# Lo weights 112 bytes into their tiles for K and Q, and a new order of the products of K, G and Q, in a two-layer linear-attention and MLP kernel

## The chip, the cores and the metric

One core of one Trainium2 chip runs the whole program. Times are device microseconds of one execution. Before the change three runs took 870.21, 870.62 and 871.27 us, median 870.62.

## The reference, cut to what matters

An input of 2048 tokens of 448 features passes twice through an attention block and an MLP block, each behind a layer norm and with a residual. The attention is linear: no softmax, a sum over all tokens of phi(k) times v, 16 heads of 28.

```
def A(x, wqkv, wo):                      # S = 2048, D = 448, H = 16, Dh = 28
    q, k, v = split(x @ wqkv)
    phi = lambda t: where(t > 0, t + 1, exp(t)) + 1e-6
    pq, pk = phi(q), phi(k)
    kv = einsum("bhsd,bhse->bhde", pk, v)
    z = einsum("bhsd->bhd", pk)
    o = einsum("bhqd,bhde->bhqe", pq, kv) / (einsum("bhqd,bhd->bhq", pq, z) + 1e-6)
    return o @ wo

def B(x, w1, b1, w2, b2):                # F = 1792
    return gelu(x @ w1 + b1) @ w2 + b2

for _ in range(2):
    x = x + A(layernorm(x), wqkv, wo)
    x = x + B(layernorm(x), w1, b1, w2, b2)
```

All is float32.

## The kernel before

**Products in pieces.** TensorE multiplies fp32r operands here. To keep the accuracy of float32, each operand is split into hi (rounded) and lo (the rest), and a product is made as hi*hi + hi*lo + lo*hi in one accumulator in PSUM. The 448 rows of a contraction are taken as three chunks of 128 and a tail of 64; in the tail the 128 rows hold hi and lo of one side, stacked, so that it needs two products and not three. A product of one tile is thus 3 x 3 + 2 = 11 matmuls.

**Which side is the weights.** Each matmul loads 128x128 weights and streams the other operand past them. For K and Q the weights are turned (transposed) tokens and the matrix streams, 448 columns; for G, which is tokens transposed times phi(k), the weights are the tokens as they are; in the MLP's second half (y) and in the output product of attention (op) they are turned activations. In the MLP's first half (hp) the matrix is the weights and 512 tokens stream.

**Phase 1.** For each layer and each of 16 tiles of 128 tokens, `phase1` (from L610) makes the layer norm, turns the tile, and issues K(t) (`stage_k`, through `proj`, L321), the transposes of tile t+1 if that tile is turned on TensorE (only tiles 0 to 7 of layer 0, `TURNED`), G(t-1) (`stage_g`, L522) and Q(t) (`stage_q`). The order within a step is written out in `STEP` and `STEPS`, one token for one stage. Q is made in the loop for tiles 0 to 8 only; the Q's of the last seven tiles fill gaps of the transition (`ORDER`, tokens Q and Qa), where K and V are combined with the output matrix.

**Other tiles are turned by VectorE and DMA.** `turn` transposes 32x32 blocks (L299, L300), `store_sq` writes two tiles to DRAM (L305) and `spread` reads them back so that the blocks are in place (L311). `split_t` (L313) then makes hi on ScalarE (XH, L317) and lo on VectorE (XL, L318). For tiles turned on TensorE this is `split_x` (L272, L273).

**Where the pieces lie.** XH and XL (class `Block`, L228) hold four tiles each, two buffers; the same tags serve the turned tokens of the MLP (key "m"), where XL streams. Tiles of tags B and F are 576 elements wide and can be used from element `APART` = 28 on, that is 112 bytes in: so lie xnl (lo of the tokens for G, L446), ql and gl. XL starts at its tile's start.

**Order of products before.** `proj` goes through the chunks: hi by the matrix's hi, hi by its lo, lo by its hi, so that lo weights come third, sixth, ninth and eleventh of eleven. G does the same for three chunks, and its last chunk has two products with hi weights, since there hi and lo of the tail share one tile: lo comes third, sixth and ninth. For the tile before the last two (`t == NT - 3`, L526) G has an order of its own, which stays.

Of the kernel before, what the change touches and what calls it, by code (L numbers as in the profile page):

```python
# [9 lines left out]
F32 = mybir.dt.float32  # L10
F32R = mybir.dt.float32r
# [11 lines left out]
def linear_attn_mlp_kernel(  # L23
# [12 lines left out]
    pe, act, dve, pool, sp = nc.tensor, nc.scalar, nc.vector, nc.gpsimd, nc.sync  # L36
# [4 lines left out]
    H, DH = 16, 28  # L41
    NT = S // 128
# [4 lines left out]
    TL = D - 64  # L47
    LAYERS = 2

    consts = ctx.enter_context(tc.tile_pool(name="consts", bufs=1))  # L50
    wts = ctx.enter_context(tc.tile_pool(name="wts", bufs=1))
    work = ctx.enter_context(tc.tile_pool(name="work", bufs=2))
# [9 lines left out]
    def bank(tag, bufs, name):  # L62
        return psum.tile([128, 512], F32, name=name, tag=tag, bufs=bufs)
# [7 lines left out]
    APART = 28  # L71
# [24 lines left out]
    wkq = {}  # L96
# [90 lines left out]
                       compare_op=OP.is_ge, fill=0.0)  # L187
    b1s = consts.tile([128, NF], F32, name="b1s")
    b2b = consts.tile([128, D], F32, name="b2b")
    consts.tile([128, 48], F32, name="space")  # L190

    w1h = wts.tile([128, 3, F], F32R, name="w1h")
    w1l = wts.tile([128, 3, F], F32R, name="w1l")
# [9 lines left out]


    def ln_bn(xs):
        st = work.tile([128, 6], F32, name="bst", tag="bst", bufs=3)
        dve.bn_stats(st, xs)
        return st

    def ln_stats(xs, st=None):  # L210
        st = ln_bn(xs) if st is None else st
        mv = work.tile([128, 2], F32, name="bmv", tag="bmv", bufs=3)
        dve.bn_aggr(mv, st)
        ve = work.tile([128, 1], F32, name="bve", tag="bve", bufs=3)
        dve.tensor_scalar(ve, mv[:, 1:2], 1e-5, None, op0=OP.add)  # L215
        rs = work.tile([128, 1], F32, name="brs", tag="brs", bufs=3)
        pool.tensor_tensor(rs, ve, mhalf, op=OP.pow)  # L217
        return xs, mv, rs

# [6 lines left out]


    class Block:  # L228
        def __init__(self):
            self.hi = work.tile([128, 2048], F32R, name="XH", tag="XH", bufs=2)  # L230
            self.lo = work.tile([128, 2048], F32R, name="XL", tag="XL", bufs=2)

        def pieces(self, t):

# [11 lines left out]
    blocks = {}  # L246

    def block(key):
        if key not in blocks:
            blocks[key] = Block()  # L250
        return blocks[key]

    tps = {}
# [1 line left out]
    def transpose_x(xn, tail, key, j, tag="m"):  # L255

        block(key)
        tp = tps[key, j] = bank(tag, 4 if tag == "acc" else 2, "tp")
        for c in range(4):
            pe.transpose(tp[:, c * 128:(c + 1) * 128], xn[:, c * 128:(c + 1) * 128] if c < 3 else tail, ident)  # L260

    def transpose_halves(xn, tail, key, j):

        block(key)
        tps[key, j] = [bank("acc", 4, "tp") for _ in range(2)]
        for c in range(4):
            pe.transpose(tps[key, j][c // 2][:, c % 2 * 128:][:, :128], xn[:, c * 128:(c + 1) * 128] if c < 3 else tail, ident)
# [26 lines left out]
    def turn(x, key, t):  # L294
        x = x[:, :D]
        if (key, t // 2) not in squares:
            squares[key, t // 2] = half("sq")
        sq = squares[key, t // 2].rearrange("p (m c u n) -> p c m u n", m=4, c=4, n=32)[:, :, :, t % 2]
        dve.transpose(sq[:, :3], x[:, :TL].rearrange("p (c m n) -> p c m n", c=3, n=32))  # L299
        dve.transpose(sq[:, 3].rearrange("p (u m) n -> p u m n", u=2),  # L300
                      x[:, TL:].rearrange("p (m n) -> p m n", n=32)[:, None].to_broadcast([128, 2, 2, 32]))

    def store_sq(key, h):
        d = stored[key, h] = dram([128, 1024], F32, f"sq_{'_'.join(map(str, key))}_{h}")
        sp.dma_start(d, squares.pop((key, h)))  # L305

    def spread(key, h):
        r = spreads[key, h] = half("sp")
        d = stored.pop((key, h)).rearrange("(i r) (m f) -> m r i f", i=4, m=4)
        for m in range(4):  # L310
            sp.dma_start(r[m * 32:(m + 1) * 32].rearrange("r (i f) -> r i f", i=4), d[m])  # L311
# [6 lines left out]
        eng.tensor_tensor(lo.rearrange("p (c i n) -> p c i n", c=4, n=32), x, f(h), op=OP.subtract)  # L318


    def proj(name, key, j, o=None, cs=range(4)):  # L321
        if o is None:
            o = bank("m" if name == "k" else "h", 2, "ps" + name)[:, :D]
        b = blocks[key]
        for c in cs:
            if c < 3:
                hi, lo = wkq[name, c]
                pe.matmul(o, b.still(b.hi, j, c), hi, start=(c == 0), stop=False)  # L328
                pe.matmul(o, b.still(b.hi, j, c), lo, start=False, stop=False)  # L329
                pe.matmul(o, b.still(b.lo, j, c), hi, start=False, stop=False)  # L330
            else:
                pe.matmul(o, b.still(b.hi, j, 3), wkq[name, 3], start=False, stop=False)
                pe.matmul(o, b.still(b.lo, j, 3), wkq[name, 3], start=False, stop=True)
        return o
# [71 lines left out]
    def stage_a(l, t):  # L406
        sts[l, t] = ln_stats(xt.pop((l, t)))
# [16 lines left out]
    def stage_sp(l, t):  # L424
        if t >= TURNED[l]:
            block(("a", l, t // 4))
            spread(("a", l, t // 4), t % 4 // 2)
# [23 lines left out]

    ko = {}

    def stage_k(l, t, cs=range(4)):
        ko[l, t] = proj("k", ("a", l, t // 4), t % 4, ko.get((l, t)), cs)

    def stage_kphi(l, t):
        o = ko.pop((l, t))
# [36 lines left out]
    qs_ = {}  # L495

    def stage_q(l, t, cs=range(4), tag=None):
        if tag:
            qs_[l, t] = bank(tag, 4, "psq")[:, :D]
        qs_[l, t] = proj("q", ("a", l, t // 4), t % 4, qs_.get((l, t)), cs)  # L500
        if 3 in cs:
            qo.append((l, t, qs_.pop((l, t))))

# [18 lines left out]
    def stage_g(l, t, acc):  # L522
        h, lo = split.pop((l, t))
        kh, kl = ks.pop((l, t))
        first, last = t == 0, t == NT - 1
        if t == NT - 3:  # L526

            for c in range(4):
                pe.matmul(acc[c], h[:, c * 128:(c + 1) * 128], kh, start=False, stop=False)
            for c in range(3):  # L530
                pe.matmul(acc[c], lo[:, c * 128:(c + 1) * 128], kh, start=False, stop=False)
            for c in range(4):
                pe.matmul(acc[c], h[:, c * 128:(c + 1) * 128], kl, start=False, stop=False)
            return
        for c in range(3):
            s = slice(c * 128, (c + 1) * 128)
            pe.matmul(acc[c], h[:, s], kh, start=first, stop=False)  # L537
            pe.matmul(acc[c], h[:, s], kl, start=False, stop=False)  # L538
            pe.matmul(acc[c], lo[:, s], kh, start=False, stop=last)
        pe.matmul(acc[3], h[:, TL:], kh, start=first, stop=False)  # L540
        pe.matmul(acc[3], h[:, TL:], kl, start=False, stop=last)

# [211 lines left out]
    def q_scale(l, b, j, tr):  # L756
        pq = pqt[l, b * 4 + j]
        pz = pzs.pop((l, b, j))
        dn = work.tile([128, H], F32, name="dn", tag="dn", bufs=2)
        dve.tensor_reduce(dn, pz.rearrange("p (h d) -> p h d", d=DH), axis=mybir.AxisListType.X, op=OP.add)  # L760
        dve.tensor_tensor(dn, dn, tr.dc, op=OP.add)
        rd = work.tile([128, H], F32, name="rd", tag="rd", bufs=2)
        dve.reciprocal(rd, dn)
        p3 = pq.rearrange("p (h d) -> p h d", d=DH)
        dve.scalar_tensor_tensor(p3, p3, 1e-6, rd[:, :, None].to_broadcast([128, H, DH]),
                                 op0=OP.add, op1=OP.mult)
# [62 lines left out]
    def m_split(l, b, j):  # L829

        if j < 2:
            split_t(("m", l, b), j, *block(("m", l, b)).pieces(j), dve if j else pool)
        else:
            split_x(("m", l, b), j)
# [150 lines left out]

    table(AF.Exp)
    stage_a(0, 0)
    work.tile([128, 32], F32, name="space", tag="space", bufs=1)
    bn = ln_bn(xt[0, 1])
    split_hi("k", 0, st_k)  # L990
    stage_n(0, 0)
# [4 lines left out]
    for l in range(LAYERS):  # L996
        tr = SimpleNamespace(mp={})
        za, acc = phase1(l, tr)
# [9 lines left out]
        def pre(j):  # L1008
# [4 lines left out]

        tok_ = SimpleNamespace(
            Q=lambda j: stage_q(l, fill.pop(0)), Qp=lambda j: fill_qphi(), Qv=lambda j: stage_qphi(j or 9),
            Qa=lambda j: stage_q(l, fill.pop(0), tag="acc"), G=lambda j: stage_g(l, NT - 1, acc),
            ld=lambda j: (load_pq(l, 0, j), load_x(l, j)), z=lambda j: trans_z(tr, zs[l]), gt=lambda j: trans_gt(tr, acc),
# [4 lines left out]
            x=lambda j: m_split(l, 0, j), tu=lambda j: turn(xns.pop(("m", l, j)), ("m", l, 0), j),  # L1022
            st=lambda j: store_sq(("m", l, 0), 0), sp=lambda j: spread(("m", l, 0), 0), pre=pre, b=biases)
        for tok in ORDER.split():
            name, j = tok.rstrip("0123456789"), int("0" + tok.lstrip("abcdefghijklmnopqrstuvwxyzQTG"))
# [6 lines left out]
        for b in range(NB):  # L1032
            acc = [bank("acc", 4, f"y{j}")[:, :D] for j in range(4)]
# [5 lines left out]
            for i in range(NF):  # L1039
# [12 lines left out]
                elif l + 1 < LAYERS:  # L1052
# [4 lines left out]
                    if i in (3, 4, 6, 7, 8):  # L1057
                        t = (3, 4, 6, 7, 8).index(i)
# [36 lines left out]
```

## Time and profile before

| | |
|---|---|
| runs | 870.21, 870.62, 871.27 us |
| profiled execution | 870.69 us, of which the span of instructions 869.0 us |
| TensorE busy | 863.5 us, 4182 matmuls (each float32 one that is not a transpose counts twice) |
| VectorE, ScalarE, GpSimd busy | 491.6, 344.7, 221.5 us |
| K, G and Q of layer 0 | from 7 to about 137 us |
| K, G and Q of layer 1 | from 438 to about 564 us |

In the rows of groups stand line, engine, operation, out<-in by the program's names, shapes and count, then busy us, mean ns of one, and the idle time of the engine ahead of them. Rows of the timeline begin with the start in us from the span's start and the duration. PE is a matmul, PEld the load of its weights, SPq a DMA issued by SyncE. Matmuls are pipelined: a record of 360 ns doesn't mean that the next starts 360 ns later.

### The profile page before, as it was taken

To read this page: it belongs to the slowest core of one execution; us is meant where nothing else is said; L and a number is where in the kernel's file an instruction comes from. 1 tells how busy PE (TensorE), PEld (TensorE's weight loads), DVE (VectorE), ACT (ScalarE), POOL (GpSimd) and SP (SyncE) were. 2 spreads that over 40 slices of the span, in tenths; PEclk is the share of its full clock that TensorE was granted. 3 is DMA by queue.
4 is the path that set the end of the run, shared out by engine and by line. 5 is a ranking of instruction groups with operands and counts; after the bars stand their busy time and mean duration, and the time that the engine had idled before them with its cause. 6 is when DMAs were issued, how large, how long until landed. Compare 5 with 4: busy or idle time off the path is not lost.

```text
span 869.0 us, 11679 instructions
## 1 busy us (share of the span) xinstructions
PE 863.5 (99%) x4182; PEld 771.0 (89%) x4182; DVE 491.6 (57%) x958; ACT 344.7 (40%) x606; POOL 221.5 (25%) x250
## 2 busy tenths in 40 slices
PE   9999999999999999999999999999999999999998
PEld 8999888888888888888899998888888888888887
DVE  6888496658456443226477876864674483533112
ACT  6776635324323322333355665342233133223231
POOL 5566532235012102012222344120220140140000
PEclk9999999999999999999999999999999999999999
DMA  5474736624313402051145443252332413111001
GB/s 160 139 234 158 210 89 205 193 89 131 134 60 105 158 0 98 1 181 49 49 145 184 165 133 106 98 182 90 105 115 92 129 68 125 49 49 42 1 1 43
DMA packets 63642, 94.76 MB, mean 109 GB/s; under 512 B 8928, under 2 KB 58720, under 8 KB 63584
## 3 DMA queue, kind: packets, MB, share of 16 engines
q1 hardware_dynamic: 63408, 93.87, 33.6%
q8 instruction: 33, 0.54, 0.3%
q14 instruction: 25, 0.20, 0.1%
q10 hardware_dynamic: 176, 0.14, 0.0%
HBM read 56.17 MB, written 34.60 MB: 104 GB/s over the span
## 4 chain that ended last, share of the span: by engine, by line
PE 98%; DMA 0%; DVE 0%; ACT 0%; POOL 0%; issue 0%; SPq 0%; DVEq 0%; ACTq 0%
PE y L895 10%; PE y L894 10%; PE y L896 10%; PE hp L863 9%; PE hp L861 9%; PE hp L862 9%; PE hp L865 3%; PE hp L864 3%; PE psk L329 2%; PE psq L329 2%; PE psq L328 2%; PE psq L330 2%; PE psk L330 2%; PE psk L328 2%; PE G L538 2%; PE G L537 2%
## 5 line engine op out<-in xcount | busy, mean ns | idle before, releaser
L871 DVE TENSOR_TENSOR gl<-g,gh 128x512 fp32r<-128x512 f32 x112 | 83.2, 743 | 294.4 <-ACT gh L870 294.4
L867 ACT ACTIVATE g<-hp,b1s 128x512 f32<-128x512 f32 x112 | 77.1, 688 | 400.9 <-PE hp L865 392.6
L895 PE MATMUL y<-w2l,gh 128*128 128x448 f32 x447 | 163.6, 366 | 0.0
L894 PE MATMUL y<-w2h,gh 128*128 128x448 f32 x447 | 162.0, 362 | 0.0
L896 PE MATMUL y<-w2h,gl 128*128 128x448 f32 x447 | 160.0, 358 | 0.0
L863 PE MATMUL hp<-XL,w1h 128*128 128x512 f32 x336 | 130.9, 390 | 0.0
L862 PE MATMUL hp<-XH,w1l 128*128 128x512 f32 x336 | 130.7, 389 | 0.0
L861 PE MATMUL hp<-XH,w1h 128*128 128x512 f32 x336 | 130.7, 389 | 0.0
L217 POOL TENSOR_TENSOR brs<-bve,mhalf 128x1 f32<-128x1 f32 x64 | 39.4, 616 | 281.0 <-DVE bve L215 277.9
L894 PEld LDWEIGHTS y<-w2h,gh 128*128 128x128 f32 x447 | 83.7, 187 | 9.4
L895 PEld LDWEIGHTS y<-w2l,gh 128*128 128x128 f32 x447 | 83.9, 188 | 7.0
L896 PEld LDWEIGHTS y<-w2h,gl 128*128 128x128 f32 x447 | 84.0, 188 | 5.0
L863 PEld LDWEIGHTS hp<-XL,w1h 128*128 128x128 f32 x336 | 63.1, 188 | 13.6 <-issue 0.6
L861 PEld LDWEIGHTS hp<-XH,w1h 128*128 128x128 f32 x336 | 63.0, 187 | 10.6
L862 PEld LDWEIGHTS hp<-XH,w1l 128*128 128x128 f32 x336 | 63.1, 188 | 9.9
L870 ACT CAST gh<-g 128x512 fp32r<-128x512 f32 x112 | 69.6, 622 | 3.6
L754 POOL TENSOR_TENSOR pz<-pq,zb 128x448 f32<-128x448 f32 x32 | 36.7, 1148 | 81.9 <-DVE dn L760 61.0
L448 POOL TENSOR_TENSOR xnl<-x,xnh 128x384 fp32r<-128x384 f32 x32 | 35.2, 1099 | 72.1 <-ACT xnh L447 40.1
L318 DVE TENSOR_TENSOR XL<-sp,XH 128x512 fp32r<-128x512 f32 x50 | 44.6, 898 | 4.3 <-ACT XH L317 4.3
L865 PE MATMUL hp<-XL,w1x 128*128 128x512 f32 x112 | 43.6, 389 | 0.0
L864 PE MATMUL hp<-XH,w1x 128*128 128x512 f32 x112 | 43.6, 389 | 0.0
L823 POOL TENSOR_TENSOR x<-x,b2b 128x448 f32<-128x448 f32 x32 | 41.9, 1331 | 0.0
(169 smaller groups left out, 1565.2 us busy)
## 6 DMA issues: line engine op xcount, KB each, us to landing
x<-in_A_x_dram SPq DMA_DIRECT2D x32, 224.0 KB, 4.0
pq_d<-eq SPq DMA_DIRECT2D x32, 224.0 KB, 2.7
pq<-pq_d SPq DMA_DIRECT2D x32, 224.0 KB, 3.3
sq_m<-sq SPq DMA_DIRECT2D x14, 512.0 KB, 2.8
sp<-sq_m SPq DMA_DIRECT2D x56, 128.0 KB, 2.8
x<-x_d SPq DMA_DIRECT2D x32, 224.0 KB, 3.4
sq_a<-sq SPq DMA_DIRECT2D x12, 512.0 KB, 2.9
sp<-sq_a SPq DMA_DIRECT2D x48, 128.0 KB, 3.1
```

Of the source, the lines that this page charges most:

```text
L318: eng.tensor_tensor(lo.rearrange("p (c i n) -> p c i n", c=4, n=32), x, f(h), op=OP.subtract)
L861: pe.matmul(o, w1h[:, c, s], x.moving(x.hi, c), start=(c == 0), stop=False)
L862: pe.matmul(o, w1l[:, c, s], x.moving(x.hi, c), start=False, stop=False)
L863: pe.matmul(o, w1h[:, c, s], x.moving(x.lo, c), start=False, stop=False)
L864: pe.matmul(o, w1x[:, s], x.moving(x.hi, 3), start=False, stop=False)
L865: pe.matmul(o, w1x[:, s], x.moving(x.lo, 3), start=False, stop=True)
L867: act.activation(g, hp, AF.Gelu_apprx_tanh, bias=b1s[:, i:i + 1])
L870: act.copy(gh, g)
L871: dve.tensor_sub(gl, g, f(gh))
L894: pe.matmul(acc[j], gh[:, s], w2h[:, i], start=first, stop=False)
L895: pe.matmul(acc[j], gh[:, s], w2l[:, i], start=False, stop=False)
L896: pe.matmul(acc[j], gl[:, s], w2h[:, i], start=False, stop=stop)
```

## The change

XL's tile becomes 64 elements wider, and blocks of attention (key "a") use it from element 28 on, blocks of the MLP from its start. The products of K and Q of a whole tile, and those of G, are put in an order by tables: a list of the hi products and one of the lo products is merged so that lo products come at given places of the eleven. Which places is given by layer and tile (`k_at`, `q_at`, `g_at`). Taken through K, G and Q of a step in which nothing stands between them, these places are every third: in layer 1, tile 3, K has lo at 2, 5, 8, 11, G at 3, 6, 9, Q at 1, 4, 7, 10. K of tiles 10 to 15 starts with lo. The parts of K and Q that are issued chunk by chunk for the first two tiles of layer 0 keep their order.

Room is found elsewhere: the small tiles of the layer norm's statistics and the denominator move to another pool, the denominator has one buffer and not two, and two unused spacers go.

```diff
-    consts.tile([128, 48], F32, name="space")
...
-        st = work.tile([128, 6], F32, name="bst", tag="bst", bufs=3)
+        st = consts.tile([128, 6], F32, name="bst", tag="bst", bufs=3)
...
     class Block:
-        def __init__(self):
+        def __init__(self, at):
             self.hi = work.tile([128, 2048], F32R, name="XH", tag="XH", bufs=2)
-            self.lo = work.tile([128, 2048], F32R, name="XL", tag="XL", bufs=2)
+            self.lo = work.tile([128, 2112], F32R, name="XL", tag="XL", bufs=2)[:, at:at + 2048]
...
-            blocks[key] = Block()
+            blocks[key] = Block(APART if key[0] == "a" else 0)
...
+    def merge(his, los, at):
+
+        his, los = iter(his), iter(los)
+        return [next(los if i + 1 in at else his) for i in range(11)]
+
-    def proj(name, key, j, o=None, cs=range(4)):
+    def proj(name, key, j, o=None, cs=range(4), at=(3, 6, 9, 11)):
         if o is None:
             o = bank("m" if name == "k" else "h", 2, "ps" + name)[:, :D]
         b = blocks[key]
+        if len(cs) == 4:
+            w = [wkq[name, c] for c in range(3)]
+            his = [(b.still(b.hi, j, c), p) for c in range(3) for p in w[c]] + [(b.still(b.hi, j, 3), wkq[name, 3])]
+            los = [(b.still(b.lo, j, c), w[c][0]) for c in range(3)] + [(b.still(b.lo, j, 3), wkq[name, 3])]
+            for i, (x, p) in enumerate(merge(his, los, at)):
+                pe.matmul(o, x, p, start=(i == 0), stop=(i == 10))
+            return o
...
+    def k_at(l, t):
+        if t < 9:
+            return ((2, 5, 8, 11) if t == 2 else (3, 6, 9, 11)) if l == 0 or t == 0 else (2, 5, 8, 11)
+        return (2, 5, 8, 11) if t == 9 else (1, 4, 7, 10)
+
+    def q_at(l, t):
+        if t < 9:
+            return (2, 5, 8, 11) if l == 0 and t < 8 else (2, 4, 7, 10) if t == 0 else (1, 4, 7, 10)
+        return (2, 5, 8, 11) if t == 10 else (3, 6, 9, 11) if t in (12, 13) else (1, 4, 7, 10)
+
+    def g_at(l, t):
+        if t < 9:
+            return (4, 7, 10) if l == 0 and t < 7 else (3, 6, 9)
+        return (4, 7, 10) if t == NT - 1 else (2, 5, 8)
...
-        for c in range(3):
-            s = slice(c * 128, (c + 1) * 128)
-            pe.matmul(acc[c], h[:, s], kh, start=first, stop=False)
-            pe.matmul(acc[c], h[:, s], kl, start=False, stop=False)
-            pe.matmul(acc[c], lo[:, s], kh, start=False, stop=last)
-        pe.matmul(acc[3], h[:, TL:], kh, start=first, stop=False)
-        pe.matmul(acc[3], h[:, TL:], kl, start=False, stop=last)
+        x = [h[:, c * 128:(c + 1) * 128] for c in range(3)] + [h[:, TL:]]
+        his = [(c, x[c], k) for c in range(4) for k in (kh, kl)]
+        los = [(c, lo[:, c * 128:(c + 1) * 128], kh) for c in range(3)]
+        made = merge(his, los, g_at(l, t))
+        for i, (c, w, k) in enumerate(made):
+            others = [m[0] for m in made[:i]], [m[0] for m in made[i + 1:]]
+            pe.matmul(acc[c], w, k, start=first and c not in others[0], stop=last and c not in others[1])
...
-        dn = work.tile([128, H], F32, name="dn", tag="dn", bufs=2)
+        dn = consts.tile([128, H], F32, name="dn", tag="dn", bufs=1)
...
-    work.tile([128, 32], F32, name="space", tag="space", bufs=1)
```

More of the change, by code (lines that the diff above doesn't have):

```diff
@@ L211, in ln_stats @@
         st = ln_bn(xs) if st is None else st
-        mv = work.tile([128, 2], F32, name="bmv", tag="bmv", bufs=3)
+        mv = consts.tile([128, 2], F32, name="bmv", tag="bmv", bufs=3)
         dve.bn_aggr(mv, st)
-        ve = work.tile([128, 1], F32, name="bve", tag="bve", bufs=3)
+        ve = consts.tile([128, 1], F32, name="bve", tag="bve", bufs=3)
         dve.tensor_scalar(ve, mv[:, 1:2], 1e-5, None, op0=OP.add)
-        rs = work.tile([128, 1], F32, name="brs", tag="brs", bufs=3)
+        rs = consts.tile([128, 1], F32, name="brs", tag="brs", bufs=3)
         pool.tensor_tensor(rs, ve, mhalf, op=OP.pow)
@@ L452, in linear_attn_mlp_kernel @@
     ko = {}
+    def k_at(l, t):
[10 more added lines that the diff above has]
+        return (4, 7, 10) if t == NT - 1 else (2, 5, 8)
     def stage_k(l, t, cs=range(4)):
-        ko[l, t] = proj("k", ("a", l, t // 4), t % 4, ko.get((l, t)), cs)
+        ko[l, t] = proj("k", ("a", l, t // 4), t % 4, ko.get((l, t)), cs, k_at(l, t))
     def stage_kphi(l, t):
@@ L499, in stage_q @@
             qs_[l, t] = bank(tag, 4, "psq")[:, :D]
-        qs_[l, t] = proj("q", ("a", l, t // 4), t % 4, qs_.get((l, t)), cs)
+        qs_[l, t] = proj("q", ("a", l, t // 4), t % 4, qs_.get((l, t)), cs, q_at(l, t))
         if 3 in cs:
```

## The prediction

> **What bounds the kernel now.** I read the page first, parts 1, 2 and 4.
>
> ```profile
> span 869.0 us, 11679 instructions
> ...
> PE 863.5 (99%) x4182; PEld 771.0 (89%) x4182; DVE 491.6 (57%) x958; ACT 344.7 (40%) x606; POOL 221.5 (25%) x250
> ...
> PEclk9999999999999999999999999999999999999999
> ...
> PE 98%; DMA 0%; DVE 0%; ACT 0%; POOL 0%; issue 0%; SPq 0%; DVEq 0%; ACTq 0%
> ```
>
> TensorE is busy all the time, at its full clock, and 98% of the chain that ended last is matmuls, so the time is the number of products times the distance from one to the next. The change removes no product. What it can change is that distance, and I looked for a place where products of the same size follow each other at two paces. The groups by line, shapes kept apart:
>
> ```profile
> L328 PE MATMUL psq<-wq,XH 128*128 128x448 f32 x96 | 35.6, 371 | 0.0
> ...
> L329 PE MATMUL psq<-wq,XH 128*128 128x448 f32 x96 | 35.1, 366 | 0.0
> L330 PE MATMUL psq<-wq,XL 128*128 128x448 f32 x96 | 35.0, 365 | 0.0
> L537 PE MATMUL G<-kh,xnh 128*128 128x448 f32 x90 | 33.4, 371 | 0.0
> ...
> L539 PE MATMUL G<-kh,xnl 128*128 128x448 f32 x90 | 32.5, 361 | 0.0
> L804 PE MATMUL op<-wq,qh 128*128 128x448 f32 x72 | 26.4, 366 | 0.0
> L803 PE MATMUL op<-wq,qh 128*128 128x448 f32 x72 | 26.1, 362 | 0.0
> L805 PE MATMUL op<-wq,ql 128*128 128x448 f32 x72 | 25.8, 358 | 0.0
> ...
> L332 PE MATMUL psq<-wq,XH 128*128 128x448 f32 x32 | 11.7, 367 | 0.0
> ```
>
> Q (psq) and the output product (op) move the same wq buffers, 448 columns past 128x128 weights, in the same order hi, hi, lo. By the code they differ in one thing: ql lies 28 elements, 112 bytes, into its tile, XL at its start. op's records last 366, 362 and 358 ns in turn, Q's 371, 366 and 365. G, whose xnl also lies 112 bytes in, stands between. The records overlap, so I take the pace from starts, in the timeline. First y, which also runs hi, hi, lo with an offset lo, then K, where one step of the loop (K, G and Q of 11 products each, 33 together) repeats:
>
> ```profile
> 302.41 0.36 PE L894 MATMUL y<-w2h,gh 128*128 128x448 f32 x1
> ...
> 304.81 0.39 PE L861 MATMUL hp<-XH,w1h 128*128 128x512 f32 x1
> ```
> ```profile
> 462.93 0.36 PE L328 MATMUL psk<-wk,XH 128*128 128x448 f32 x1
> ...
> 496.33 0.36 PE L328 MATMUL psk<-wk,XH 128*128 128x448 f32 x1
> ```
>
> Twelve products of y take 2.40 us, 200 ns each. Five steps, 165 products, take 33.40 us, 202.4 ns each. So there are 2.4 ns a product to be had in K, G and Q. The same order of G is found at two paces:
>
> ```profile
> 51.69 0.36 PE L539 MATMUL G<-kh,xnl 128*128 128x448 f32 x1
> ...
> 52.29 0.36 PE L539 MATMUL G<-kh,xnl 128*128 128x448 f32 x1
> ...
> 52.89 0.36 PE L539 MATMUL G<-kh,xnl 128*128 128x448 f32 x1
> ```
> ```profile
> 76.30 0.36 PE L539 MATMUL G<-kh,xnl 128*128 128x448 f32 x1
> ...
> 76.91 0.36 PE L539 MATMUL G<-kh,xnl 128*128 128x448 f32 x1
> ...
> 77.53 0.36 PE L539 MATMUL G<-kh,xnl 128*128 128x448 f32 x1
> ```
>
> From lo to lo it is 0.60 us here (200 ns a product) and 0.615 there (205 ns), within one G each: an offset lo at every third place gives a cycle that keeps itself, and whether it is the good or the bad one is settled by how the sequence is entered. The change puts the offset into K and Q and lines up the three products so that the cycle need not be entered again each time.
>
> **The change part by part.** K and Q have 3x96 and 2x32 products each over both layers (x96 and x32 above), 352, and G as many, one for each of K's; 1056 in all.
>
> Layer 1's loop, nine full steps and seven of K and G alone: some 430 products. With lo exactly at every third place through K, G and Q I take y's 200.0, that is 2.4 ns less. In the seven later steps 22 products hold 7 lo's, so one distance is four; that breaks the cycle once a step, and I take 2.2 ns over the whole: 430 x 2.2 = 0.95 us.
>
> Layer 0's loop up to the K of tile 9: seven steps have four transposes between K and G. G after them is in the good cycle already (the rows at 51.69), so only K and Q gain, 22 products x 2.4, less what K's last three lose on the way into the transposes: 0.055 us a step, 0.4 in seven. The two steps without transposes gain 33 x 2.4 = 0.08 each, of which I count 0.1 together. Sum 0.5 us.
>
> Layer 0 from there to the K of tile 14 is held by something else:
>
> ```profile
> 91.29 0.19 PEld L328 LDWEIGHTS psk<-wk,XH 128*128 128x128 f32 x1
> ...
> 91.84 0.19 PEld L330 LDWEIGHTS psk<-wk,XL 128*128 128x128 f32 x1
> ...
> 93.97 0.50 PEld L529 LDWEIGHTS G<-kh,xnh 128*128 128x128 f32 x3 [0.41 <-ACT kh L465]
> ```
> ```profile
> 91.50 0.36 PE L328 MATMUL psk<-wk,XH 128*128 128x448 f32 x1
> ...
> 91.91 0.40 PE L330 MATMUL psk<-wk,XL 128*128 128x448 f32 x1
> ```
> ```profile
> 91.09 0.69 DVE L318 TENSOR_TENSOR XL<-sp,XH 128x512 fp32r<-128x512 f32 x1 [2.40 <-ACT XH L317]
> ```
> ```profile
> 90.44 0.62 ACT L317 CAST XH<-sp 128x512 fp32r<-128x512 f32 x1 [2.49 <-DMA sp<-sq_a]
> ```
> ```profile
> 85.72 1.75 SPq L311 DMA_DIRECT2D sp<-sq_a  x4
> ```
>
> XL of tile 14 is finished at 91.78, because its turned tokens come late from the DMA issued at 85.72; the load of the first lo weights waits to 91.84 for it. ACT's queue is held by the same DMA, so its kh for G of tile 13 is late too, and PE waits 0.41 us there. TensorE coming sooner doesn't move these: the 88 products of four steps after the K of tile 9 gain 0.2 us that I count at nothing, the late XL being their cover; without it they are worth 0.2 more. Here the change also puts lo first in K, two products sooner. Its load would be due at about 91.29 and still goes at 91.84, so K's first product starts where its third did, 0.4 us later, with all of K queued behind it on PE, and behind K its Relu and Exp, and G. G is then due 0.4 us later too, which is the 0.41 us that its loads now wait for kh: that wait falls away. A product after a late load comes soon behind it (91.91 after 91.84, where 91.50 after 91.29 shows the usual 0.2), so a wait of 0.4 us costs PE less than 0.4. From both sides: 0 lost if the wait gives all back, 0.4 if nothing; I take 0.1 lost, near the row of the wait.
>
> The other K's of tiles 10 to 15 have lo first too. In layer 1 there is room:
>
> ```profile
> 503.05 0.82 DVE L318 TENSOR_TENSOR XL<-sp,XH 128x512 fp32r<-128x512 f32 x1
> ```
> ```profile
> 505.26 0.36 PE L328 MATMUL psk<-wk,XH 128*128 128x448 f32 x1
> ```
>
> XL is done 1.4 us ahead of K, and two products are 0.4. Tile 15 of layer 0 is near its limit:
>
> ```profile
> 95.02 1.14 DVE L318 TENSOR_TENSOR XL<-sp,XH 128x512 fp32r<-128x512 f32 x1
> ```
> ```profile
> 96.31 0.36 PE L328 MATMUL psk<-wk,XH 128*128 128x448 f32 x1
> ```
>
> XL ends at 96.16, K's first load is due 0.2 ahead of 96.31, at 96.1; K starting 0.1 later by the loss above, the two meet. It costs from 0 to 0.1; I take 0.
>
> After the loops: G of tile 15 and seven Q's in each layer, in layer 0 K of tile 15 and a G more: 110 and 88 products between transposes and other products. At 2.3 ns 0.25 and 0.2 us. The first two tiles of layer 0 keep the old order but get the offset; 30 products there are not behind a wait, 0.06 us.
>
> Nothing is charged for the rest. DVE writes gl 112 bytes in already and takes no longer for it, and it idles 43%; dn with one buffer is written and read by DVE alone, in order; the statistics only move in SBUF.
>
> ```profile
> L871 DVE TENSOR_TENSOR gl<-g,gh 128x512 fp32r<-128x512 f32 x112 | 83.2, 743 | 294.4 <-ACT gh L870 294.4
> ...
> L318 DVE TENSOR_TENSOR XL<-sp,XH 128x512 fp32r<-128x512 f32 x50 | 44.6, 898 | 4.3 <-ACT XH L317 4.3
> ```
>
> Sum: 0.95 + 0.5 - 0.1 + 0.25 + 0.2 + 0.06 = 1.86 us less. The profiled execution took 870.69 us (869.0 of span and 1.7 around it), 0.07 above the median of the three runs, 870.62; so 868.8.
>
> **A rule against it.** op's lo at 358 ns against Q's at 365, on the same moving tiles, says that the place of the weights matters. The Trainium skill, page "SBUF — State Buffer", section "Who interferes with whom", gives TensorE two independent read ports, one for the moving operand and one for weights, and its "Specifications (TRN2)" speak of 16-byte lines, of which 112 bytes are a whole number. By that page the offset could change nothing, and the sum would be that of the third rival below. The rows speak against it, but they compare different stages.
>
> **The rivals.** First, slower: the bad cycle. If the long sequence is entered as G was at 76.30, it stays there, since nothing breaks it any more; 205 in place of 202.4 ns over some 900 products in loops and tails is +2.3 us, 872.9. With a share f in the bad cycle the change is 2.4(1-f) - 2.6f a product, so it turns slower from f = 0.48 on. For it: that stretch. Against: y, op and most of G after transposes are found in the good one.
>
> Second, the good cycle is lost at each boundary, or at each break of three, and found again only after several products, as in G now; half the gain, 0.9 us, 869.7. For it: K's late lo and the transposes break it for certain. Against: in layer 1's nine full steps nothing stands between K, G and Q.
>
> Third, the offset does nothing in K and Q and what differs between Q and op is something else of their stages. Then only order changes, and with the 0.1 us of tile 14 it is 870.7. Against it G, which stands between K and Q in the same stage and has the 361 ns.
>
> **How the numbers follow.** Forecast 0.64, bad cycle 0.08, half 0.22, nothing 0.06. What a measurement can tell from no change is about 0.2%, 1.74 us, so the line is at 868.9, close to the forecast. Its own spread is from 868.0 (2.4 ns on all 1056 products, and 0.1 for the rest) to 869.4; I put four fifths of it under the line: 0.51, the rest of it with the second and third rival and half of the first within: 0.45; slower 0.04. The range 868.0 to 870.3 takes in the second rival and leaves out the first and most of the third.
>
> **What would show it.** Starts of psk rows 6.60 us apart in layer 1's full steps in place of 6.68; mean records of the lo products of K and Q at 358 ns; G's 371 down to 362 to 366. The load of the first lo weights of tile 14 waiting for XL, and the wait for kh after it shorter. The bad cycle would show as lo to lo 0.61 us over whole steps; the third rival as steps that stay at 6.68. A new wait of PE for XL elsewhere, or steps that gain while the span doesn't, would prove me wrong on what covers what.

## The result, and the profile after

| | before | after |
|---|---|---|
| runs, median | 871.07 us (869.93 to 872.39, 22 runs) | 869.54 us (868.91 to 870.74, 22 runs) |
| profiled execution | 870.69 us | 869.28 us |
| its span | 869.0 us | 867.5 us |

The ratio of the times is 0.9985, with a 95% interval of 0.9978 to 0.9991: about 1.3 us less. Parts 1 and 4 of the page of after:

```profile
span 867.5 us, 11673 instructions
...
PE 862.3 (99%) x4182; PEld 771.1 (89%) x4182; DVE 492.0 (57%) x958; ACT 345.0 (40%) x606; POOL 221.9 (26%) x250
...
PE 96%; DVE 1%; DMA 1%; ACT 1%; issue 0%; POOL 0%; SPq 0%; DVEq 0%; ACTq 0%; POOLq 0%
```

The same 4182 products keep TensorE busy for 1.2 us less. The chain that ended last has 1% each of DMA, ScalarE and VectorE in it, which were at 0%: on its way back it now leaves TensorE at one place, which is K of tile 14 in layer 0, below. K and Q have one line now, so the groups part by hi and lo (columns as before: busy us, mean ns of one, idle ahead):

```profile
L334 PE MATMUL psq<-wq,XL 128*128 128x448 f32 x120 | 43.7, 364 | 0.0
...
L334 PE MATMUL psk<-wk,XL 128*128 128x448 f32 x120 | 43.3, 361 | 0.3 <-DVE XL L317 0.3
...
L567 PE MATMUL G<-kh,xnl 128*128 128x448 f32 x90 | 32.3, 359 | 0.0
```

These means mix good stretches and bad ones. The pace is in the starts. The first products of the same two K's of layer 1, five steps apart, in the timeline of after:

```profile
462.17 0.37 PE L334 MATMUL psk<-wk,XH 128*128 128x448 f32 x1
...
495.17 0.37 PE L334 MATMUL psk<-wk,XH 128*128 128x448 f32 x1
```

33.00 us where it was 33.40: 6.60 a step, 200.0 ns a product. And a K from within, lo after lo:

```profile
462.97 0.36 PE L334 MATMUL psk<-wk,XL 128*128 128x448 f32 x1
...
463.57 0.36 PE L334 MATMUL psk<-wk,XL 128*128 128x448 f32 x1
...
464.17 0.36 PE L334 MATMUL psk<-wk,XL 128*128 128x448 f32 x1
```

0.60 us from lo to lo throughout, the good cycle of the prediction: behind a lo the next products start after 196, 199 and 205 ns. By stage, from the starts of K in both traces (K2 is the first product of K of tile 2, hp the first product of the MLP):

| stretch | before, us | after, us | difference |
|---|---|---|---|
| start of span to K2, layer 0 | 20.07 | 19.93 | -0.14 |
| K2 to K9, layer 0 | 49.13 | 48.80 | -0.33 |
| K9 to K15, layer 0 | 27.10 | 27.07 | -0.03 |
| K15 to hp, layer 0 | 41.31 | 41.31 | 0.00 |
| hp to K0 of layer 1 | 300.78 | 300.83 | +0.05 |
| K0 to K15, layer 1 | 84.69 | 83.73 | -0.96 |
| K15 to hp, layer 1 | 41.32 | 41.25 | -0.07 |
| hp of layer 1 to end of span | 304.57 | 304.62 | +0.05 |

Two thirds of the gain come from layer 1's loop. The two stretches of the MLP, which the change leaves as they were, take 300.74 to 300.85 and 304.54 to 304.65 us over the kernels here (three executions apart, named below), so 0.05 us there says nothing. Two stretches show the bad cycle in place of the good one. One begins with the G behind a dummy transpose in the step of tile 7 and lasts through G(6), Q(7) and K(8), 57.5 to 64.3 us; three lo's of K(8), in the timeline of after:

```profile
62.48 0.36 PE L334 MATMUL psk<-wk,XL 128*128 128x448 f32 x1
...
63.10 0.36 PE L334 MATMUL psk<-wk,XL 128*128 128x448 f32 x1
...
63.71 0.36 PE L334 MATMUL psk<-wk,XL 128*128 128x448 f32 x1
```

0.61 to 0.62 us from lo to lo (about 203, 203 and 208 ns), 204.6 ns a product over Q(7) and over K(8), each of which had some 202.6 before. The other is the Q's of tiles 12 and 13 in both layers, behind op. The first product of a Q and the first of op after it, in the timeline of after and then of before:

```profile
124.88 0.57 PE L334 MATMUL psq<-wq,XH 128*128 128x448 f32 x2
...
127.14 0.37 PE L818 MATMUL op<-Mh,qh 112*128 112x448 f32 x1
```
```profile
125.39 0.37 PE L328 MATMUL psq<-wq,XH 128*128 128x448 f32 x1
...
127.62 0.36 PE L792 MATMUL op<-Mh,qh 112*128 112x448 f32 x1
```

The eleven products take 2.25 us where they took 2.23, and the twelve of op behind them 202.8 ns each, where it was 200.2. So the tails give back there what other Q's gain.

Tile 14 of layer 0, the rows of ScalarE, VectorE, the weight loads and TensorE in the timeline of after:

```profile
89.84 0.62 ACT L316 CAST XH<-sp 128x512 fp32r<-128x512 f32 x1 [2.43 <-DMA sp<-sq_a]
```
```profile
90.49 0.69 DVE L317 TENSOR_TENSOR XL<-sp,XH 128x512 fp32r<-128x512 f32 x1 [2.35 <-ACT XH L316]
```
```profile
91.23 0.19 PEld L334 LDWEIGHTS psk<-wk,XL 128*128 128x128 f32 x1 [0.67 <-DVE XL L317]
...
93.36 0.80 PEld L555 LDWEIGHTS G<-kh,xnh 128*128 128x128 f32 x4
```
```profile
91.24 0.47 PE L334 MATMUL psk<-wk,XL 128*128 128x448 f32 x1 [0.29 <-DVE XL L317]
```

The first load of K, now lo, waits 0.67 us for XL, which ends at 91.18 because XH waited for the DMA; G's loads after it wait for kh no more (0.41 us before).

### The profile page after: what moved, and what is told of

Same layout as the page of the kernel before. It is cut to its first block, busy times and chain, and to the rows that moved or that the text cites. A ratio compares the mean times of both kernels' runs of the same rounds, so it can differ in the third digit from the quotient of the medians.

```text
span 867.5 us, 11673 instructions
## 1 busy us (share of the span) xinstructions
PE 862.3 (99%) x4182; PEld 771.1 (89%) x4182; DVE 492.0 (57%) x958; ACT 345.0 (40%) x606; POOL 221.9 (26%) x250
## 4 chain that ended last, share of the span: by engine, by line
PE 96%; DVE 1%; DMA 1%; ACT 1%; issue 0%; POOL 0%; SPq 0%; DVEq 0%; ACTq 0%; POOLq 0%
PE y L921 10%; PE y L920 10%; PE y L922 10%; PE hp L889 9%; PE hp L887 9%; PE hp L888 9%; PE psq L334 8%; PE psk L334 6%; PE G L567 6%; PE hp L890 3%; PE hp L891 3%; PE op L830 2%; PE op L829 2%; PE op L831 2%; PE op L819 1%; PE op L818 1%
## 5 line engine op out<-in xcount | busy, mean ns | idle before, releaser
L334 PE MATMUL psq<-wq,XH 128*128 128x448 f32 x210 | 62.2, 365 | 0.0
L334 PE MATMUL psk<-wk,XH 128*128 128x448 f32 x210 | 61.9, 364 | 0.0
L567 PE MATMUL G<-kh,xnh 128*128 128x448 f32 x120 | 44.5, 371 | 0.0
```

The lines of the kernel that those rows point to most:

```text
L334: pe.matmul(o, x, p, start=(i == 0), stop=(i == 10))
L567: pe.matmul(acc[c], w, k, start=first and c not in others[0], stop=last and c not in others[1])
```

## The experiments

All traces below were read in the same way: first products of K of layer 1's tiles 4 and 9 (five steps, 165 products), and the table's stretches. Three executions (at16, bad_entry, dummies3) are some 0.5 us longer in each of two stretches, with no cause in their edits: K15 to hp of layer 0 (41.75 to 41.82 us, where the same stretch of layer 1 takes 41.24 to 41.31) and hp to K0 of layer 1 (301.35 to 301.39 us). So single times are not compared, the loops are.

### The two parts alone: offset_only and order_only

The first keeps XL 112 bytes in and goes back to the old places of lo; the second keeps the new order and puts XL at its start.

```diff
     def k_at(l, t):
+        return (3, 6, 9, 11)
...
     def q_at(l, t):
+        return (3, 6, 9, 11)
...
     def g_at(l, t):
+        return (3, 6, 9)
```

> XL 112 bytes in for K and Q, but K, G and Q in the order of before (lo third, sixth, ninth, and eleventh in K and Q). Theory (offset and unbroken every-third together): K and Q now have lo, one hi, lo at their end, which breaks the cycle twice a step, so it is left and found again; a full step of layer 1 (33 products) takes 6.62 to 6.66 us, between 6.60 of the changed kernel and 6.68 of before, and about half of the gain is left: some 0.8 us less than before. Rival that the offset alone does it: steps of 6.60 and at least the whole gain, 1.5 us, since K of tile 14 also doesn't wait longer. Rival that the order alone does it: 6.68, no gain.

```diff
-            blocks[key] = Block(APART if key[0] == "a" else 0)
+            blocks[key] = Block(0)
```

> The new order of K, G and Q with XL at its tile's start again. Theory: only G has offset lo weights, 3 of 33, so nothing keeps the cycle over K and Q: a full step of layer 1 stays within 6.66 to 6.70 us, K and Q at 202 to 203 ns a product, and the time is that of before or up to 0.3 us over it, because the wait of K of tile 14 for XL stays two products earlier. Rival that the order alone does it: 6.60 us a step and 1.5 us less than before.

offset_only: 870.83 us over 11 runs, ratio 0.9994 (0.9985 to 1.0003). order_only: 870.75 us over 11 runs, ratio 0.9997 (0.9988 to 1.0006). Neither can be told from no change by time alone; the traces part them. The first products of the two K's, offset_only and then order_only:

```profile
462.79 0.57 PE L334 MATMUL psk<-wk,XH 128*128 128x448 f32 x2
...
496.09 0.57 PE L334 MATMUL psk<-wk,XH 128*128 128x448 f32 x2
```
```profile
462.49 0.36 PE L334 MATMUL psk<-wk,XH 128*128 128x448 f32 x1
...
495.89 0.36 PE L334 MATMUL psk<-wk,XH 128*128 128x448 f32 x1
```

The offset alone gives 33.30 us, a quarter of the 0.40 that the change brings here (over the whole loop of layer 1 84.39 us against 84.69, a third); the order alone 33.40, which is nothing, and with it the tiles that were moved to make room are worth nothing here, since order_only has them moved too. So the third rival falls: the place of the weights matters. And the old places of lo, where the distance from lo to lo is two at the end of K and Q and five from G to Q, lose most of it, more than the half that was expected. The gain needs both parts.

### Is it the 112 bytes? at32, at16, at24

The order of the change, with XL 128, 64 and 96 bytes in.

```diff
-            blocks[key] = Block(APART if key[0] == "a" else 0)
+            blocks[key] = Block(32 if key[0] == "a" else 0)
```

at16 and at24 have 16 and 24 in that place.

> The changed kernel with XL 32 elements, 128 bytes, in and not 112. Theory (what counts is where in a line of 128 bytes or less the lo weights begin, against hi): as XL at 0, steps of 6.66 to 6.70 us. Rival (any place other than the tile's start, or a place away from XH, is enough): 6.60 us.

> The changed kernel with XL 16 elements, 64 bytes, in. If a line of 64 bytes or less is what counts, as XL at 0: 6.66 to 6.70 us a step; if one of 128 bytes, another value, 6.60 if every shift helps.

> The changed kernel with XL 24 elements, 96 bytes, in. 0 and 128 bytes gave 202.5 ns a product in K and Q, 64 gave 204, 112 gives 200. If the good place is a narrow one just ahead of the line's end: 202 to 204, steps of 6.66 to 6.72. If all of the last quarter is good: 200, steps of 6.60.

One run each: 870.31, 872.33 and 870.76 us. Their first products of K, at32, at16 and at24 in turn:

```profile
462.75 0.36 PE L334 MATMUL psk<-wk,XH 128*128 128x448 f32 x1
...
496.02 0.36 PE L334 MATMUL psk<-wk,XH 128*128 128x448 f32 x1
```
```profile
464.35 0.36 PE L334 MATMUL psk<-wk,XH 128*128 128x448 f32 x1
...
497.89 0.36 PE L334 MATMUL psk<-wk,XH 128*128 128x448 f32 x1
```
```profile
462.74 0.36 PE L334 MATMUL psk<-wk,XH 128*128 128x448 f32 x1
...
496.27 0.36 PE L334 MATMUL psk<-wk,XH 128*128 128x448 f32 x1
```

33.27, 33.54 and 33.53 us. By operand, mean distance of the products of layer 1's full steps:

| XL begins at | K, ns | Q, ns | five steps, us |
|---|---|---|---|
| 0 bytes (order_only) | 202.7 | 202.6 | 33.40 |
| 64 | 204.4 | 203.6 | 33.54 |
| 96 | 204.4 | 204.1 | 33.53 |
| 112 (the change) | 200.0 | 199.5 | 33.00 |
| 128 | 202.5 | 202.2 | 33.27 |

128 bytes act on K and Q nearly as none do, while G, whose xnl is 112 bytes in throughout, goes to 200.2 ns beside them (202.3 in order_only). 64 and 96 bytes are worse than no offset. That isn't a matter of the entry alone: in both, G comes back to about 0.60 us from lo to lo in each step, and the Q and K behind it lose it again. So it isn't enough that lo is shifted or lies apart from hi; where it begins counts. That 0 and 128 are alike fits a period of 128 bytes, but this is one pair. The places are counted from the tile's start: whether the address itself counts or the distance from hi isn't shown, and which of the places not tried are as good stays open.

### Lo first at tile 14: k14_third

```diff
     def k_at(l, t):
+        if (l, t) == (0, 14):
+            return (3, 6, 9, 11)
```

> The changed kernel, but K of tile 14 of layer 0 has its lo weights third, sixth, ninth and eleventh. Theory (lo first moves a wait that was there to the start of K, and most of it is given back at the wait for kh): the 0.67 us for which the weight loads idle before K goes, a wait of 0.2 to 0.4 us comes back at G of tile 13, and K of tile 15 starts 0.05 to 0.2 us sooner against K of tile 9 than in the changed kernel. Rival that lo first costs all of the wait: 0.4 us or more sooner. Rival that the late XL costs the same wherever it is waited for: no difference over 0.05 us.

One run, 869.38 us. From the end of XL of tile 14 to the first product of K(15) it is 4.53 us, against 4.62 in after: lo first costs 0.09 us there. The wait for kh is back, as expected, and another is new. The weight loads of k14_third, and XL of tile 15 on VectorE:

```profile
93.58 0.70 PEld L557 LDWEIGHTS G<-kh,xnh 128*128 128x128 f32 x4 [0.38 <-ACT kh L493]
...
94.91 0.79 PEld L561 LDWEIGHTS G<-kl,xnh 128*128 128x128 f32 x4
95.82 0.19 PEld L334 LDWEIGHTS psk<-wk,XL 128*128 128x128 f32 x1
```
```profile
94.63 1.13 DVE L317 TENSOR_TENSOR XL<-sp,XH 128x512 fp32r<-128x512 f32 x1
```

The load for K(15), lo first too, was due at 95.71, right behind G's, and goes at 95.82, after XL ends at 95.76. So what K(14) gains, K(15) can take only in part: XL of tile 15 is next in line. K9 to K15 is 26.78 us against 27.07 in after, but 0.19 of that is tokens of tile 14 that landed sooner after K9 (its XH starts at 20.91 us, in after at 21.10), and this moves between 20.7 and 21.4 us over the executions in which SyncE issues all four DMAs.

### Is the cycle settled by its entry? bad_entry, dummies3, dummies4

bad_entry puts into the step of tile 2 of layer 1 the dummy transpose ahead of G that stood before the bad stretch in layer 0, with K(2) in the order that it had there.

```diff
     def k_at(l, t):
+        if (l, t) == (1, 2):
+            return (3, 6, 9, 11)
...
+        (1, 2): "qp K T X s a kp n kh kl tu D G bg Q ld sp",
```

> The changed kernel with one dummy transpose put between K and G of tile 2 of layer 1, as stands at tile 8 of layer 0, where the changed kernel went into the cycle of 203, 208 and 203 ns, and with K of that tile in the order of tile 8's K (lo third, sixth, ninth, eleventh). Theory (the cycle keeps itself, good or bad, and the entry decides): G of that step is entered in the bad cycle and it lasts: the full steps of layer 1 after it take 6.74 to 6.76 us in place of 6.60, for the six steps up to the last Q of the loop 0.8 to 1.0 us in all, beside about 0.15 us for the transpose itself. Rival (the good cycle is found again within a product): steps of 6.60 to 6.62 after the one with the transpose.

A miss. The first products of K(2), K(3) and K(4) in its timeline:

```profile
450.04 0.57 PE L334 MATMUL psk<-wk,XH 128*128 128x448 f32 x2
...
456.78 0.37 PE L334 MATMUL psk<-wk,XH 128*128 128x448 f32 x1
...
463.38 0.37 PE L334 MATMUL psk<-wk,XH 128*128 128x448 f32 x1
```

The step with the transpose takes 6.74 us, the next 6.60 already. Here G has lo at 3, 6 and 9 behind the transpose, in the bad stretch at 4, 7 and 10: the number of hi products between the disturbance and the first lo differs. That made the next theory, which is about this number. dummies3 puts three products with hi weights (into a bank of PSUM that nothing reads) ahead of K(2) of layer 1, so that five hi's stand between two lo's; dummies4 puts four.

```diff
+        (1, 2): "qp E K T X s a kp n kh kl tu G bg Q ld sp",
...
+                elif tok == "E":
+                    o, x = bank("h", 2, "turn")[:, :D], blocks["a", l, t // 4]
+                    for _ in range(3):
+                        pe.matmul(o, x.still(x.hi, t % 4, 0), wkq["k", 0][0], start=True, stop=True)
```

> The changed kernel with three extra products (448 columns past hi weights of tile 2, result unused) ahead of K of tile 2 of layer 1; the one extra transpose tried before had been followed by the good cycle, so this is the entry as K and G had it before the change: a lo after five hi in a row. In the traces so far such a lo, after distances of 199, 207, 202, 203 ns, is reached by 208 ns and followed by 202 and 203. Theory: the bad cycle begins there and lasts to the end of the full steps, since nothing breaks it: 6.74 to 6.76 us a step for tiles 2 to 8, in all 0.6 us for the products and 0.8 to 1.0 us for the cycle, seen as the distance from K of tile 2 to K of tile 10. Rival (the good cycle comes back by itself within a step or two): 0.6 us and at most 0.2.

> As the run with three extra products, with four, so that six hi stand ahead of the lo. Theory (the entry alone decides): in the traces so far the distance from the sixth hi to lo is 203 and the next 207 and 205, then 196: the good cycle within three or four products, steps of 6.60; so four extra products cost 0.8 to 0.9 us, some 0.6 us less than three do. Rival (extra products cost what they take): 0.2 us more than with three.

The added products, the two K's, and between them three lo's of K(4), in the timeline of dummies3; then the same without the lo's in dummies4:

```profile
449.96 0.77 PE L671 MATMUL turn<-wk,XH 128*128 128x448 f32 x3
...
464.07 0.37 PE L334 MATMUL psk<-wk,XH 128*128 128x448 f32 x1
...
464.89 0.36 PE L334 MATMUL psk<-wk,XL 128*128 128x448 f32 x1
...
465.50 0.36 PE L334 MATMUL psk<-wk,XL 128*128 128x448 f32 x1
...
466.12 0.36 PE L334 MATMUL psk<-wk,XL 128*128 128x448 f32 x1
...
497.80 0.37 PE L334 MATMUL psk<-wk,XH 128*128 128x448 f32 x1
```
```profile
449.03 0.98 PE L671 MATMUL turn<-wk,XH 128*128 128x448 f32 x4
...
463.06 0.37 PE L334 MATMUL psk<-wk,XH 128*128 128x448 f32 x1
...
496.06 0.37 PE L334 MATMUL psk<-wk,XH 128*128 128x448 f32 x1
```

33.73 us in dummies3, 33.00 in dummies4, with the same code in all these steps. Three more products hold the bad cycle for every full step behind them, tiles 2 to 8, at 6.747 us a step and 204.4 ns a product; four leave the good one. From K(1) to K(10), three cost 1.74 us over after and four 0.83: adding the fourth saves 0.9 us. This is the first rival, made on purpose, and its mechanism and price are real (it said 205 ns). But it doesn't last whatever comes: in dummies3 the bad cycle ends at 506.8 us, where the new order first has a distance of four, from G(9) to the lo at the start of K(11), and the good one follows. From six hi's the good cycle follows, from five the bad, in one execution each; what in TensorE keeps either of them isn't shown.

### Versions made from this: better, better2, better3

better aims at the bad stretches and at tile 14. It moves lo in the Q's of tiles 12 and 13, gives K(14) its old order, and changes Q(8) and G(7) of layer 0.

```diff
     def k_at(l, t):
+        if (l, t) == (0, 14):
+            return (3, 6, 9, 11)
...
     def q_at(l, t):
+        if (l, t) == (0, 8):
+            return (2, 5, 8, 10)
...
-        return (2, 5, 8, 11) if t == 10 else (3, 6, 9, 11) if t in (12, 13) else (1, 4, 7, 10)
+        return (2, 5, 8, 11) if t == 10 else (2, 5, 8, 11) if t in (12, 13) else (1, 4, 7, 10)
...
-            return (4, 7, 10) if l == 0 and t < 7 else (3, 6, 9)
+            return (4, 7, 10) if l == 0 and t < 8 else (3, 6, 9)
```

> The changed kernel with the stretches that its trace shows in the bad cycle entered in another way: tile 8 of layer 0 (G of tile 7 with lo at 4, 7, 10, Q of tile 8 at 2, 5, 8, 10) and the Q's of tiles 12 and 13 of both layers (2, 5, 8, 11 in place of 3, 6, 9, 11), and K of tile 14 of layer 0 with lo third. Theory: those Q's go from 204.7 to 201 or 202 ns a product, Q of tile 8 and K of tile 9 from 204.6 to 200.5; 0.2 us in the Q's with the output products behind them, 0.1 at tile 8 (in part hidden by the late XL of tile 14), 0.1 at tile 14: 0.3 to 0.4 us less than the changed kernel, 1.8 to 2.0 us less than before. Rival (an entry that isn't measured is as likely bad as good): within 0.1 us of the changed kernel.

869.34 us over 11 runs, ratio 0.9981 (0.9972 to 0.9990). Its edits in the loop missed: the stretch is G(6), Q(7) and K(8), and I had changed the products after it; K2 to K9 is 48.84 us, against 48.80. The Q's behind op gained as little: Q(12) went to 201.3 ns, but the op behind it to 204.6, and the two tails are 41.25 and 41.23 us, which better3 has without this edit (41.25 and 41.24). better2 goes for the right products, and leaves Q(12) and Q(13) alone:

```diff
     def k_at(l, t):
+        if l == 0 and t in (8, 14):
+            return (2, 5, 8, 11) if t == 8 else (3, 6, 9, 11)
...
     def q_at(l, t):
+        if (l, t) == (0, 7):
+            return (1, 4, 7, 10)
...
-            return (4, 7, 10) if l == 0 and t < 7 else (3, 6, 9)
+            return (4, 7, 10) if l == 0 and t < 6 else (3, 6, 9)
```

> The changed kernel with the bad stretch after the dummy transpose of layer 0 taken out where it really stands, at G of tile 6, Q of tile 7 and K of tile 8 (G with lo at 3, 6, 9, Q at 1, 4, 7, 10, K at 2, 5, 8, 11; the try before had moved their neighbours), and lo third in K of tile 14 of layer 0. Theory: G after the transpose settles in the good cycle as in the kernel before (207, 204, 207, 204, 203, 199, 205, 196), and Q and K follow it at 200: 0.12 to 0.17 us by K of tile 9; and 0.09 us at tile 14, since K of tile 15 starts 4.53 us after the end of tile 14's XL where lo is third and 4.62 where it is first, in all runs so far. Together 0.2 to 0.25 us less than the changed kernel, 1.7 to 1.9 less than before.

869.25 us over 11 runs, ratio 0.9981 (0.9972 to 0.9990). Q(7) and K(8) are at 199.5 and 200.1 ns, and K2 to K9 is 48.68 us: the bad stretch had cost 0.12. What is left in layer 0 is the DMA for tile 14. better3 is better2 with two of the four DMAs that bring back the tokens of tiles 12 to 15 issued by ScalarE instead of SyncE, in the step of tile 12.

```diff
+        last = (key, h) == (("a", 0, 3), 1)
...
-            sp.dma_start(r[m * 32:(m + 1) * 32].rearrange("r (i f) -> r i f", i=4), d[m])
+            def go(eng, m=m):
+                eng.dma_start(r[m * 32:(m + 1) * 32].rearrange("r (i f) -> r i f", i=4), d[m])
+            if last and m >= 2:
+                rest.append(go)
+            else:
+                go(sp)
...
+        (0, 12): "qp K T X s kp S kh kl G sp bg",
...
+                elif tok == "S":
+                    while rest:
+                        rest.pop(0)(act)
```

> As the run before it, with two of the four DMAs that bring the turned tokens of tiles 14 and 15 of layer 0 issued by ScalarE after its second exponential of the step, in place of by SyncE after the other two. Theory (from K of tile 9 to K of tile 15 nothing but this landing counts): XH of tile 14 starts 0.4 to 0.8 us sooner against K of tile 9, and K of tile 15 starts 26.4 to 26.6 us after K of tile 9 in place of 27.0: 0.4 us less than without, the 0.2 us of the faster products among it. Rival: ScalarE's issues delay kh of the step and G by as much, or the landing isn't what counts: 26.9 to 27.2 us.

868.90 us over 8 runs, ratio 0.9976 (0.9966 to 0.9986). The issues, then what they release, and K(14), in the timeline of better3:

```profile
84.94 0.80 SPq L313 DMA_DIRECT2D sp<-sq_a  x2
```
```profile
84.89 0.87 ACTq L313 DMA_DIRECT2D sp<-sq_a  x2
...
88.74 0.62 ACT L323 CAST XH<-sp 128x512 fp32r<-128x512 f32 x1 [1.68 <-DMA sp<-sq_a]
```
```profile
90.45 0.57 PE L341 MATMUL psk<-wk,XH 128*128 128x448 f32 x2
...
90.86 0.36 PE L341 MATMUL psk<-wk,XL 128*128 128x448 f32 x1
```

Both engines issue at once, and XH starts 3.80 us after SyncE's first issue, where in after it was 4.43 (85.41 to 89.84) and in the other executions 4.26 to 4.81; XL is done at 90.08 and no product of K(14) waits. Tile 15 comes sooner with it, and K(15) waits no more either. K9 to K15 is 26.55 us, as expected, but against 26.70 in better2 and 27.07 in after: 0.15 us less than without the edit, where 0.4 was expected; six steps of 22 products at 200 ns would be 26.4. XH of tile 14 starts 20.34 us after K9, in better2 20.84, in after 21.10; so 0.26 of the 0.37 us by which better2 is ahead of after there is the landing in that execution, and not its edit. better3 has the lowest median of the kernels here, though its interval overlaps those of after and better2.

## Why the prediction was nearly right, and what it sized wrongly

It forecast 1.86 us less, 868.8. The span of the profiled execution went down by 1.5, the runs by about 1.3 to 1.5; 869.54 lies in the range. It leaned a little to a gain of over 0.2% and the gain is 0.15%. Step by step:

- **Layer 1's loop, 0.95 us: 0.96 measured.** The pace of 200.0 ns, read from y before, holds in K to the tenth; Q is faster still (199.5) and G slower (200.5). That isn't a cost of a boundary: every distance in a full step is three, and the eleven products of each hold other shares of 196, 199 and 205 ns. The distance of four stands in the later steps alone; the five from K(9) to K(14) take 4.405 to 4.414 us where 22 products at 200.0 ns are 4.40, so it costs 0.01 us a step or less. That the sum agrees to 0.01 us is in part luck: there are eight full steps, not nine, and they gained 2.6 ns a product where 2.4 was taken, the later ones 2.2. offset_only and order_only show that it is both parts together, and the third rival, that the offset does nothing, is wrong.
- **Layer 0 to K(9), 0.5 us: 0.33 measured from K(2) to K(9).** This holds five of the seven steps with four transposes, and they gained 0.33 us, 0.066 each; the prediction's 0.055 is less than that, and yet more than its own terms give (22 x 2.4 ns is 0.053, before anything is taken off). That mainly K and Q gain there is right: K takes 2.21 us and Q 2.20 in place of 2.23 each, G 2.29 in place of 2.30. Taken wrongly is that the two steps without four transposes gain 0.1 as well: together they gained nothing, since the one with a dummy transpose falls into the bad cycle for 33 products. better2 takes this away and gets 0.12 us back.
- **K(9) to K(15): 0.2 counted as nothing, and 0.1 lost.** K9 to K15 changed by 0.03 us, with XL of tile 14 ending 0.13 sooner after K9 (22.58 us and 22.45) and 0.10 lost behind it: the cover is real, k14_third measures the loss at 0.09, and better3, which brings the tokens sooner, uncovers the gain. The wait for kh fell away as said, and that XL of tile 15 and K(15) would just meet is what k14_third shows.
- **The tails, 0.45 us: 0.07 measured, the largest error.** This term was mis-sized. It multiplied 198 products by 2.3 ns, as if a Q between other products always entered the good cycle. Two Q's in each layer enter the bad one behind op, lose 0.02 us each, and carry op behind the first of them from 200.2 to 202.8 ns; the two zp products of a layer take 0.06 us longer. The second rival, by which the cycle is lost at each boundary, had a chance of 0.22; its mechanism is nearest to what the tails show, but they keep less than a sixth of their gain and not half.
- **The launch, 0.06 us:** can't be read. K(2) begins 0.14 us sooner, but from 19.69 to 20.64 us over the kernels here, several of which do not differ up to there.
- **What would show it.** Steps of 6.60 and the load that waits for XL came as said, and K's lo records have a median of 358 ns in layer 1. That G's 371 ns would fall was wrong, though its starts are closer:

```profile
L567 PE MATMUL G<-kh,xnh 128*128 128x448 f32 x120 | 44.5, 371 | 0.0
```

The records of hi products of G stayed at 371 ns while its starts closed up from 202.4 to 200.5 ns, so a record's length doesn't give the pace. (The records of op, 366, 362 and 358 ns in the prediction, are in the order of its lines 362, 366 and 358.)

The Trainium skill, page "SBUF — State Buffer", section "Who interferes with whom", gives TensorE two independent read ports, one for the moving operand and one for weights. The prediction read from this that the offset could change nothing; the measured 200.0 against 202.7 ns (offset with order, order without) differs from that reading, and the measurement decides.

## What to carry to other kernels

Where products of one size run at two paces in one trace, look at the starts and at where the weights lie, and take the distance from a stage that already has the good pace; over the long undisturbed loop here it held to the tenth of a nanosecond. Don't multiply it into short stretches between other work: which cycle a stretch is in depends on how it was entered, and 33 products cost more here than before. And count a gain ahead of a late transfer as nothing until the transfer itself is earlier.

## What the runs showed of the hardware that was not expected

- The distance between products with 128x128 weights and 448 columns depends on where the lo weights begin, counted from their tile's start: 200.0 ns in K at 112 bytes, 202.5 to 202.7 at 0 and 128, 204.4 at 64 and at 96.
- The two cycles keep themselves: after three added products 6.747 us a step for as long as nothing breaks the sequence, after four 6.60, the rest of the code being the same.
- A fourth added product can be cheaper than its absence: from K(1) to K(10) three added products cost 1.74 us, four 0.83.
